# Where the loads of the third batch's keys and values stand in the queue of SP

## The chip, the core and the metric

The kernel runs on one core of a Trainium2 chip. The core has a TensorE for matmuls (PE in the profile, PEld for its weight loads), a VectorE (DVE), a ScalarE (ACT), a GpSimd (POOL), and SyncE (SP), which here does nothing but issue DMAs. Each engine runs its own list of instructions in order and waits on semaphores for the others. The metric is the device time of one execution in microseconds (us), lower is better; the time of a kernel is the median over its runs.

## What is computed

Two blocks in a row. The first is an attention with polynomial features: for each of 4 batches and 4 heads, 1088 tokens of 32 numbers; the second is a mixture of 4 experts, each of two weight matrices with a relu between, over the 4352 tokens that the first one leaves.

```python
def phi(x):                                   # 32 numbers -> 64 features
    a = np.einsum('rd,bhsd->bhsr', S1, x)     # S1, S2: 8 x 32
    b = np.einsum('rd,bhsd->bhsr', S2, x)
    return np.einsum('bhsi,bhsj->bhsij', a, b).reshape(*x.shape[:-1], 64)

q_p, k_p = phi(q), phi(k)
kv = np.einsum('bhsf,bhsd->bhfd', k_p, v)     # over all tokens of a batch
z = np.sum(k_p, axis=2)
attn = np.einsum('bhsf,bhfd->bhsd', q_p, kv) / (np.einsum('bhsf,bhf->bhs', q_p, z)[..., None] + 1e-06)
x = attn.transpose(0, 2, 1, 3).reshape(4352, 128)

p = domain_probs / (domain_probs.sum(-1, keepdims=True) + 1e-09)
out = sum(p[:, e:e+1] * (np.maximum(x @ w1[e], 0) @ w2[e]) for e in range(4))
```

## The kernel before

**The main loop is the mixture.** The 4352 tokens are cut into chunks (128, 448, 512, then seven of 448, and 128 at the end). For each chunk the loop at the end of the kernel goes through 16 steps: 4 experts times 4 pairs of blocks of the inner dimension; step `i` is step `i % 16` of chunk `i // 16`. A step has two halves, and a half step of an ordinary chunk is three matmuls into one PSUM bank (L1135, L1136, and L1186, between which ScalarE rescales the bank, L1137), the relu on ScalarE (L1189 or L1194), and second matmuls that are due by then (L1235, L1254). In the last step of an expert the sum is taken out of PSUM by VectorE, multiplied by the gate on GpSimd (L1293, L1295), and the next gate row is loaded into one of two buffers (L369, mostly on SP's queue).

**The attention is spread into that loop.** The queries of a batch are cut into units (first batch: 128, 448 and 512 tokens; third: 448, 448, 192). `lay_plan` (L817) writes a list of pieces with estimated costs, which the loop works off as the steps leave room. For a unit the pieces are:

- a transpose of its queries (L580);
- its projection, `unit_project` (L756): a few matmuls, a copy on ScalarE (L771), a write of the result to DRAM (`qd`, two DMAs, L773), and loads that read it back with rows repeated, as factors `qp` (L780) and `qb`. In the first batch each `qb` is loaded by four DMAs of 32 partitions each (L785), in later ones by one DMA (L782);
- the products of the factors on VectorE (`unit_product`, L791; L794), two per unit;
- the visit (`unit_visit`, L796): first the projection of the next unit, and then this unit's matmuls of products and key sums on TensorE;
- inverse, scale and a transpose to `y` on VectorE, a store of it to DRAM (`xd`, four DMAs, L728) and a load from there into `ring` (L737), where the mixture's next chunk reads its tokens; ScalarE and VectorE split these into parts (L909, L912).

In this list the third unit of the first batch is the first one made this way. Its factors are loaded in the order qp, four qb, qp, four qb.

**The keys of a batch** are pieces too (`key_pieces`, L512): transposes of `kn` (L396, L401), projections, additions (`summed`, with a copy of the values `vn` by `value_copy`), and products. `kn` and `vn` have one buffer each. `load_batch` (L137) issues the loads of the next batch's rows into them on SP's queue: one DMA of 544 KB for k, and for v four of 128 KB and two of 16 KB. The first batch is loaded at the start; the second at step 5 of the loop; the third from the last `summed` of the second batch's keys, and the fourth from that of the third's. The second batch's keys are worked on while the first chunks of the mixture run, so the third batch's load stands in SP's queue directly behind the ten DMAs of the third unit's factors, and ahead of a gate load and of the next unit's write to `qd`.

All of these DMAs are issued by SP in the order in which the program is written out. A DMA takes the eight completion semaphores in turn, and before it is issued it waits until the DMA that had the same semaphore, eight places before, has landed.

Of the kernel before, what the change touches and what calls it, by code (L numbers as in the profile page):

```python
# [24 lines left out]
def kernel(  # L25
# [28 lines left out]
    B, H, S, D = q.shape  # L54
# [48 lines left out]
    def psum(pool, tag):  # L103
        return pool.tile([P, 512], F32, tag=tag, name=tag)


    def load_rows(src, b, name, part=slice(0, S)):

        d = kn if name == "kn" else qn
        if b not in d:  # L110
            d[b] = lpool.tile([P, S], F32, tag=name, name=name)
        c, n = part.start, part.stop - part.start
        base = src.offset + b * H * S * D
        if name == "qn" and b == B - 1:
            for c, n, t in ((0, (G - 4) * D, 0), ((G - 4) * D, 4 * D, S - P)):
                nc.sync.dma_start(d[b][:, c : c + n], bass.AP(src.tensor, base + t * D, [[S * D, H], [n, 32], [1, n]]))
        else:
            nc.sync.dma_start(d[b][:, part], bass.AP(src.tensor, base + c, [[G * D, P], [1, n]]))  # L118

    def load_v(b):  # L120
        t = lpool.tile([P, H * NT * D], F32, tag="vn", name="vn")
        base = v.offset + b * H * S * D
        for a in range(4):
            nc.sync.dma_start(
                _ap(t, 32 * a, 32, 0, [[8 * D, H], [1, 8 * D]]),
                bass.AP(v.tensor, base + 8 * a * D, [[G * D, 32], [S * D, H], [1, 8 * D]]),
            )
        for a in range(2):
            nc.sync.dma_start(
                _ap(t, 32 * a, 32, 1024, [[D, H], [1, D]]),  # L130
                bass.AP(v.tensor, base + (32 + a) * D, [[G * D, 32], [S * D, H], [1, D]]),
            )
        return t
# [3 lines left out]
    def load_batch(b):  # L137
        load_rows(k, b, "kn")
        vn[b] = load_v(b)
# [254 lines left out]
    def key_turn(b, r, t0=0, n=4):  # L394
        if r < 2:
            nc.vector.transpose(  # L396
                _ap(kT, 0, P, 512 * r + P * t0, [[P, n], [32, 4], [1, 32]]),
                _ap(kn[b], 0, P, P * r + 32 * t0, [[32, n], [8 * D, 4], [1, 32]]),
            )
        else:  # L400
            nc.vector.transpose(kT[:, 1024:S], kn[b][:, 1024:S])  # L401

    def value_copy(b):
        copy = nc.gpsimd.tensor_copy if b == 1 else nc.scalar.copy
        for r in range(2):
            copy(
                vx[:, 4 * r : 4 * r + 4, :, 0:D].rearrange("p t h d -> p h t d"),
                _ap(vn[b], 0, P, P * r, [[8 * D, H], [D, 4], [1, D]]),
            )
            yield  # L410
        copy(vx[0:64, 8, :, 0:D], _ap(vn[b], 0, 64, 1024, [[D, H], [1, D]]))
# [21 lines left out]
    def key_project_wide(b, gi, kf):  # L433

        t0, n = FG[gi]
        if gi == 0:
            fss[b] = apool.tile([P, 2, NT, 32], F32, tag="fs", name="fs")
            kps[b] = apool.tile([P, NT, 2, P], F32, tag="kp", name="kp")
        for t in range(n):
            nc.tensor.matmul(  # L440
                kf[:, P * t : P * t + P], kT[:, P * (t0 + t) : P * (t0 + t + 1)], sk[:, :], start=True, stop=True
            )
        nc.scalar.copy(
            _ap(fss[b], 0, P, 32 * t0, [[32 * NT, 2], [32, n], [1, 32]]), _ap(kf, 0, P, 0, [[32, 2], [P, n], [1, 32]])
        )

    def key_add(b, gi, kf):
        t0, n = FG[gi]
        fs = _ap(fss[b], 0, P, 32 * t0, [[32 * NT, 2], [32, n], [1, 32]])
        nc.vector.tensor_tensor(out=fs, in0=_ap(kf, 0, P, HP, [[32, 2], [P, n], [1, 32]]), in1=fs, op=ALU.add)  # L450

    def key_product(b, t0, n, p, x, eng, kf=None):

        if b:
            fs = lambda k, dims: _ap(fss[b], 0, P, 32 * (NT * p + t0) + R2 * x + k, [[32, n]] + dims)
            eng.tensor_tensor(
                out=_ap(kps[b], 0, P, 256 * t0 + P * p + R * x, [[256, n], [R2, R], [1, R]]),
                in0=fs(0, [[1, R], [0, R]]), in1=fs(R, [[0, R], [1, R]]), op=ALU.mult,
            )
            return  # L460
        src, off = (kf, P * p) if kf is not None else (fss[b], 32 * (NT * p + t0))
        eng.tensor_tensor(  # L462
            out=_ap(kps[b], 0, P, 256 * t0 + P * p + 64 * x, [[256, n], [32, 2], [R, 4], [1, R]]),
            in0=_ap(src, 0, P, off + 4 * x, [[32, n], [R2, 2], [1, 4], [0, R]]),
            in1=_ap(fss[b], 0, P, 32 * (NT * p + t0) + R, [[32, n], [R2, 2], [0, 4], [1, R]]),
            op=ALU.mult,
        )
# [37 lines left out]
    def held(x):  # L505
        holds[0] += 1
        return x

    def free(n=1):
        holds[0] = max(0, holds[0] - n)  # L510

    def key_pieces(b):  # L512

        for r in range(3):
            add(0.69 if r < 2 else 0.23, lambda r=r: key_turn(b, r), f"turn{r}")
        values, kf = value_copy(b), {}

        def project(gi):
            kf[gi] = held(psum(ps_h, "h"))
            key_project_wide(b, gi, kf[gi])  # L520

        def summed(gi):
            key_add(b, gi, kf[gi])
            free()
            next(values, None)
            if gi == 2 and b + 1 < B:
                load_batch(b + 1)

        for gi in range(3):
            add(0.1, lambda gi=gi: project(gi), f"project{gi}", (f"turn{gi}", 2))  # L530
            add(0.2 if gi == 2 else 0.42, lambda gi=gi: summed(gi), f"sum{gi}", (f"project{gi}", 1))
        for p in range(2):
            for x in range(2):
                add(0.76, lambda p=p, x=x: key_product(b, 0, NT, p, x, nc.vector), "products")
# [278 lines left out]
    def add(cost, run, name, after=None):  # L813

        plan.append((cost, run, name, after))
# [597 lines left out]
    for i in range(len(steps) + LA):  # L1413
        if i < len(steps):
            m, kq = steps[i]
            until_there(START[m] + CHUNKS[m])
            rate = max(
                [0]
                + [
                    (needed[c] - spent[0]) / max(sum(rooms[2 * i : 2 * NQ * c - (EARLY if c > 1 else 13)]), 0.3)  # L1420
                    for c in range(m + 1, NC)
                    if 2 * NQ * c - (EARLY if c > 1 else 13) > 2 * i
                ]
            )

            def work():

                now[0] += 1
                if not NQ <= i < NQ + 2:
                    credit[0] = min(credit[0] + rate * rooms[min(now[0], len(rooms) - 1)], 0.5)  # L1430
                if holds[0]:
                    credit[0] = max(credit[0], 0.01)
                while credit[0] > 0:
                    cost = piece()
                    credit[0] -= cost
                    if not cost:
                        break
                for part in at_half.get(now[0] - 1, ()):
                    part()

            first(i, work, lambda j: behind(2 * i + j))
            to_due(i)
            if kq == NQ - 4 and 0 < m < NC - 2:
                until_there(START[m + 1] + CHUNKS[m + 1])
            for part in to_part.get(i, ()):
                part()
            if i == 2:
                gate_quotients()
            elif i == 8:
                later_weights()  # L1450
            elif i == 5:
                load_batch(1)
            elif i == 12:
                gate_rows()
            elif i == 13:
                later_mask()
                store_gates(range(1))
            elif i in (18, 20):
                load_gates(1, [(i - 18) // 2], nc.gpsimd)
            elif 14 <= i < 14 + B - 1:  # L1460
                store_gates(range(i - 13, i - 12))
            if m == NC - 2 and kq == NQ // 2:
                until_there(B * S)
                load_last()
        if i == LA:

            made_hp[3] = psum(ps_h, "h")
            for c in (0, HP):
                half_columns(3, made_hp[3], c)
        if NQ * (NC - 1) <= i < NQ * (NC - 1) + 2:  # L1470
            continue
        if not behind(2 * i + 1):
            next(ending, None)
# [29 lines left out]
```

## Time and profile before

| | us |
|---|---|
| median of 3 runs | 450.82 |
| lowest and highest run | 450.54, 452.36 |
| the profiled execution | 452.65 |
| its span, from the first instruction to the last | 450.9 |
| idle time of TensorE in the span | 7.9 |

TensorE's granted clock was 1.000 over the whole span. A profile gives, for each engine, its busy time, and ahead of an instruction the idle time of its engine with the thing that ended it. A wait for several semaphores is put down to the one that came last by the profile's reckoning, which can be wrong between DMAs. The DMA rows show when SP issued a DMA, not when its data landed.

This is SP's queue from the projection of the third unit's factors to the ring load of the same unit; columns: start in us, us taken, engine, line, operation, tiles (to <- from), count.

```profile
34.76 1.16 SPq L773 DMA_DIRECT2D qd<-qs  x2
35.96 0.58 SPq L118 DMA_DIRECT2D qn<-in_q_dram  x1
37.53 0.58 SPq L780 DMA_DIRECT2D qp<-qd  x1
38.16 2.64 SPq L785 DMA_DIRECT2D qb<-qd  x4
40.85 0.57 SPq L780 DMA_DIRECT2D qp<-qd  x1
41.46 3.38 SPq L785 DMA_DIRECT2D qb<-qd  x4
...
53.76 1.46 SPq L773 DMA_DIRECT2D qd<-qs  x2
56.89 0.58 SPq L780 DMA_DIRECT2D qp<-qd  x1
57.52 0.64 SPq L782 DMA_DIRECT2D qb<-qd  x1
58.28 0.54 SPq L780 DMA_DIRECT2D qp<-qd  x1
58.86 0.59 SPq L782 DMA_DIRECT2D qb<-qd  x1
60.15 1.75 SPq L728 DMA_DIRECT2D xd<-y  x4
65.12 0.34 SPq L737 DMA_DIRECT2D ring<-xd  x1
```

Between the two groups stand k and v of the third batch and one gate load.

### The profile page before, as it was taken

How to read it: one execution, taken by the hardware profiler on the slowest of the kernel's cores; microseconds unless marked ns; L12 is line 12 of the kernel's file. 1: busy time of each engine (PE TensorE's matmuls, PEld its weight loads, DVE VectorE, ACT ScalarE, POOL GpSimd, SP SyncE). 2: the span in 40 equal slices, each digit the busy share in tenths (PEclk: the TensorE clock that was granted, in tenths of full speed). 3: DMA queues.
4: the chain of work that ended last, by engine and by line, in shares of the span. 5: the costliest groups of instructions: out<-in, count | busy, mean ns of one | idle time of the engine just before them, and what ended most of it. 6: DMA issues, size and time to landing. Idle time of an engine off the chain costs nothing.

```text
span 450.9 us, 8672 instructions
## 1 busy us (share of the span) xinstructions
PE 443.0 (98%) x3021; PEld 369.0 (82%) x3021; DVE 359.5 (80%) x608; ACT 332.2 (74%) x702; POOL 122.1 (27%) x211
## 2 busy tenths in 40 slices
PE   8999899999999999999999999999999999999996
PEld 5887678777778888888888888888888888888885
DVE  5998689887988896889889868787788787876742
ACT  4478678677877876788687777887788788888831
POOL 7356123211323141212312402134123212322320
PEclk9999999999999999999999999999999999999999
DMA  6956741014223403242241152410321021027301
GB/s 196 309 133 172 164 141 32 26 36 122 93 59 87 119 23 81 52 126 74 72 118 23 22 130 65 119 43 21 95 62 30 22 47 39 22 42 253 113 4 28
DMA packets 53620, 38.47 MB, mean 85 GB/s; under 512 B 26920, under 2 KB 49640, under 8 KB 53576
## 3 DMA queue, kind: packets, MB, share of 16 engines
q1 hardware_dynamic: 52776, 37.31, 31.2%
q0 software_dynamic: 576, 0.53, 0.6%
q8 instruction: 24, 0.39, 0.4%
q14 instruction: 20, 0.16, 0.1%
q10 hardware_dynamic: 224, 0.07, 0.1%
HBM read 32.68 MB, written 5.21 MB: 84 GB/s over the span
## 4 chain that ended last, share of the span: by engine, by line
PE 92%; DMA 4%; DVE 3%; SPq 0%; issue 0%; ACT 0%; DVEq 0%; ACTq 0%
PE o L1254 40%; PE h L1186 13%; PE h L1135 13%; PE h L1136 13%; PE h L245 7%; PE o L245 3%; DMA vn<-in_v_dram 2%; DMA qb<-qd 2%; PE o L1235 2%; PE h L440 1%; DVE qp L593 1%; DVE qa L884 0%; DVE rd L625 0%; DVE kp L462 0%; SPq L118 0%
## 5 line engine op out<-in xcount | busy, mean ns | idle before, releaser
L1137 ACT ACTIVATE h<-h 128x448 f32<-128x448 f32 (+1 forms) x288 | 155.4, 540 | 79.0 <-PE h L1136 74.3
L1163 DVE SCALAR_TENSOR_TENSOR hb<-h,ha 128x448 fp32r<-128x448 f32 (+1 forms) x204 | 125.8, 624 | 54.7 <-ACT ha L1189 53.6
L1135 PE MATMUL h<-xa,wa 128*128 128x448 f32 (+1 forms) x288 | 134.6, 467 | 0.0
L1166 DVE SCALAR_TENSOR_TENSOR hd<-ha,hb 128x896 fp32r<-128x896 f32 (+1 forms) x102 | 116.4, 1141 | 8.2
L1189 ACT ACTIVATE ha<-h 128x448 fp32r<-128x448 f32 (+1 forms) x204 | 111.6, 547 | 0.0
L1186 PE MATMUL h<-xd,wd 128*128 128x448 f32 (+1 forms) x288 | 107.1, 372 | 0.1
L1136 PE MATMUL h<-xb,wb 128*128 128x448 f32 (+1 forms) x288 | 106.0, 368 | 0.0
L1293 POOL TENSOR_TENSOR ev<-ev,gate 128x256 f32<-128x256 f32 (+1 forms) x54 | 41.4, 768 | 220.0 <-DVE ev L1286 201.3
L1254 PE MATMUL o<-ha,vab 128*128 128x448 f32 (+1 forms) x204 | 76.4, 374 | 0.0
L1135 PEld LDWEIGHTS h<-xa,wa 128*128 128x128 f32 x288 | 54.2, 188 | 19.8 <-issue 15.2
L1136 PEld LDWEIGHTS h<-xb,wb 128*128 128x128 f32 x288 | 54.2, 188 | 19.3 <-issue 15.4
L1254 PE MATMUL o<-hid,w_sb 128*128 128x448 f32 (+1 forms) x136 | 62.9, 544 | 0.0
L1186 PEld LDWEIGHTS h<-xd,wd 128*128 128x128 f32 x288 | 54.0, 187 | 9.4 <-ACT h L1137 2.1
L1254 PE MATMUL o<-hd,vd 128*128 128x448 f32 (+1 forms) x204 | 58.8, 369 | 0.0
L1254 PE MATMUL o<-hb,vb 128*128 128x448 f32 (+1 forms) x136 | 49.8, 368 | 0.0
L1194 ACT ACTIVATE hid<-h 128x448 f32<-128x448 f32 (+1 forms) x84 | 46.4, 553 | 0.9 <-PE h L1186 0.8
L1295 POOL TENSOR_TENSOR total<-total,ev 128x256 f32<-128x256 f32 (+1 forms) x54 | 45.0, 833 | 4.2
L1254 PEld LDWEIGHTS o<-ha,vab 128*128 128x128 f32 x204 | 38.3, 188 | 4.2 <-issue 0.2
L1254 PEld LDWEIGHTS o<-hd,vd 128*128 128x128 f32 x204 | 38.1, 188 | 3.5
L1293 POOL TENSOR_TENSOR total<-ev,gate 128x256 f32<-128x256 f32 (+1 forms) x18 | 12.2, 698 | 74.8 <-issue 57.2
L1254 PEld LDWEIGHTS o<-hid,w_sb 128*128 128x128 f32 x136 | 25.6, 188 | 2.3
L1254 PEld LDWEIGHTS o<-hb,vb 128*128 128x128 f32 x136 | 25.5, 188 | 2.0
(142 smaller groups left out, 438.1 us busy)
## 6 DMA issues: line engine op xcount, KB each, us to landing
gate<-gates SPq DMA_DIRECT2D x22, 224.0 KB
kn<-in_k_dram SPq DMA_DIRECT2D x4, 544.0 KB
vn<-in_v_dram SPq DMA_DIRECT2D x16, 128.0 KB
w_last<-in_moe_w_dram SPq DMA_DIRECT2D x4, 512.0 KB
w_sb<-in_moe_w_dram SPq DMA_DIRECT2D x3, 512.0 KB
w_sb<-in_moe_w_dram SPq DMA_DIRECT2D x6, 256.0 KB
qp<-qd SPq DMA_DIRECT2D x6, 224.0 KB
qb<-qd SPq DMA_DIRECT2D x6, 224.0 KB
```

The costliest lines, as they stand in the source:

```text
L245: nc.tensor.matmul(out(s), weights(s), moving(s), **flags)
L1135: nc.tensor.matmul(g, wa[:, e, w], xa, start=True, stop=False)
L1136: nc.tensor.matmul(g, wb[:, e, w], xb, start=False, stop=True)
L1137: nc.scalar.activation(g, g, ACTF.Copy, scale=1.0 + R12)
L1163: nc.vector.scalar_tensor_tensor(out=hb, in0=g, scalar=0.0, in1=high, op0=ALU.max, op1=ALU.subtract)
L1166: nc.vector.scalar_tensor_tensor(out=d2, in0=a2.bitcast(F32), scalar=R12, in1=b2.bitcast(F32), op0=ALU.mult, op1=ALU.subtract)
L1186: nc.tensor.matmul(g, w, x, start=False, stop=True, skip_group_check=True)
L1189: nc.scalar.activation(ha, g, ACTF.Relu, scale=NEAR)
L1194: nc.scalar.activation(hid[i][j], g, ACTF.Relu)
L1254: nc.tensor.matmul(acc[m, e][o][:, 0:n], w, h, start=first_one, stop=last)
L1293: nc.gpsimd.tensor_tensor(out=to[:, x], in0=ev[:, x], in1=g[:, x], op=ALU.mult)
L1295: nc.gpsimd.tensor_tensor(out=total[m][:, x], in0=total[m][:, x], in1=ev[:, x], op=ALU.add)
```

## The change

The load of the third batch's rows is taken out of the keys' pieces and issued from the loop, at step 24. The fourth batch's load stays where it was, in the third batch's keys.

```diff
@@ -523,7 +523,7 @@
             key_add(b, gi, kf[gi])
             free()
             next(values, None)
-            if gi == 2 and b + 1 < B:
+            if gi == 2 and 1 < b < B - 1:
                 load_batch(b + 1)
 
         for gi in range(3):
@@ -1450,6 +1450,8 @@
                 later_weights()
             elif i == 5:
                 load_batch(1)
+            elif i == 24:
+                load_batch(2)
             elif i == 12:
                 gate_rows()
             elif i == 13:
```

Written out, SP's queue changes in one place: the seven DMAs of the third batch's k and v come twelve places later, behind one gate load, the two writes and four loads of the next unit's factors, the four stores of `y` and the ring load, and ahead of the three gate loads that follow. The instructions of the other engines stay in the same order with the same shapes; they wait for other counts of the DMA semaphores.

## The prediction

> **What bounds the kernel now.** First the busy times (part 1 of the page), then the waits between engines, then the chain that ended last and the queue of SP around the one wait that the chain shows, and last the stretches of one us there.
>
> ```profile
> PE 443.0 (98%) x3021; PEld 369.0 (82%) x3021; DVE 359.5 (80%) x608; ACT 332.2 (74%) x702; POOL 122.1 (27%) x211
> ...
> PE h L245 <- POOL sr L298: 1.3, 1, 1.3
> ...
> PE h L245 <- DVE qp L794: 1.1, 1, 1.1
> ```
>
> TensorE is busy for 98% of the span of 450.9 us, so only what fills one of its gaps, or opens a new one, moves the end. The list of waits has four columns of meaning: who waited, for whom, us in total, times, longest. Two waits of TensorE are over 1 us: 1.3 us at the start, which this change doesn't reach, and 1.1 us before matmuls of L245 for a product on VectorE (L794). Behind 54 us no wait of TensorE itself of over 0.1 us is listed. The 1.1 us is thus about all that work in the queues can win.
>
> Where that product's own time goes stands in the chain of waits:
>
> ```profile
> 42.11 8.26 DMA qb<-qd
> ...
> 50.38 2.08 DMA vn<-in_v_dram
> 52.47 0.70 DVE qp L794
> ...
> 53.21 0.69 PE h L245 x16
> ```
>
> The chain names a v load as the last releaser. The product reads qp and qb only, and the orders of SP's queue say what truly came last. SP uses eight DMA semaphores in turn, so each DMA is issued once the one eight places before it has landed. The unit's factors are qp, qb 1 to 4, a second qp and qb 5 to 8 (64 KB each qb), then comes k. So k here stands eight places behind qb 2, and each v one further:
>
> ```profile
> 45.12 0.35 SPq L118 DMA_DIRECT2D kn<-in_k_dram  x1
> ...
> 45.77 0.37 SPq L124 DMA_DIRECT2D vn<-in_v_dram  x1
> ...
> 47.82 0.31 SPq L124 DMA_DIRECT2D vn<-in_v_dram  x1
> ...
> 52.43 0.35 SPq L369 DMA_DIRECT2D gate<-gates  x1
> ```
>
> Read as landings of the DMA eight places before, with the issues between them that the same timeline has (46.97, 48.89, 50.38, 51.65): qb 2, 3 and 4 by 45.12, 45.77 and 46.97; the second qp at 47.82; qb 5 to 8 at 48.89, 50.38, 51.65 and 52.43. The product begins at 52.46, when qb 8 is there. So the last 64 KB of factors are late, not v. The steps between landings tell more: 0.65 us from qb 2 to qb 3, before any row of k moves, and (52.43 - 47.82) / 4 = 1.15 us for each of the last four, while k and v move.
>
> ```profile
> 45.00:46.00 1.00, 1.00 (x5) 1.00 0.27 102
> 46.00:47.00 1.00, 1.00 (x7) 1.00 0.95 177
> ...
> 49.00:50.00 1.00, 1.00 (x5) 1.00 1.14 165
> 50.00:51.00 1.00, 1.00 (x8) 1.00 1.09 191
> ```
>
> The last two columns are the DMA engines' mean busy share and GB/s. From 45 to 46, with qb alone, 0.27 of 16 engines (4.3 of them) move 102 GB/s. From 46 on the share is about 1 or over, yet at 49 to 51 only 165 to 191 GB/s flow: every packet takes longer.
>
> **The change part by part.** SP's program keeps its 179 rows; seven of its DMAs move: k (544 KB), four of v (128 KB) and two of v (16 KB), 1.09 MB in all, from behind qb 8 to behind the store and the ring load of the same unit. Orders and shapes of the instructions of the other four engines stay. No DMA or wait is added.
>
> (a) *The place that they leave.* The last factors must now travel without 1.09 MB beside them. At the 102 GB/s of the row for 45 to 46, one qb (65,536 B) takes 0.64 us, which is the 0.65 us seen there between landings. Slow bound: the second qp lands at 47.82 as before, and four qb follow at 0.65 us: 47.82 + 2.6 = 50.42. Fast bound: from 45.77 on there remain qb 4, the quarter of the second qp (256 KB) that lies on the same four engines if it is spread evenly (64 KB), and qb 5 to 8, six times 64 KB or 393 KB, which at 102 GB/s take 3.86 us: 49.63. If k and v cost the factors nothing, 52.43 stays; that is the bound on the other side. I take 50.4, the slower of the two without k and v: part of what held the loads up to 47.82 may have been the second qp and not k.
>
> What has to be met: TensorE ends its first half of the visit's matmuls at 52.11 (1.10 us before 53.21), and the product needs 0.75 us from its start (52.46) to TensorE's (53.21). So the product must begin by 51.36. At 50.4 it is there 0.9 us early, and TensorE's wait of 1.10 us is gone whole: **-1.10 us**. Each us by which qb 8 comes later than 51.36 gives one back.
>
> VectorE's 3.5 us of idle time before the product shrinks to some 1.5 us, and its next items (weight splits, L912) start up to 2 us earlier; TensorE doesn't wait for them (the wait list has none), so this is worth nothing.
>
> (b) *The DMAs that move up.* The gate load of L369, which SP issued at 52.43, now waits for POOL to free its tile: POOL's product with the older gate runs from 49.02 to 50.30, so it is issued near 50.35. The query write of the next unit (L773) waits for ScalarE's copy, which ends at 52.04; it was issued at 53.76 and 54.73, and now goes at about 52.1 and 52.7. Its factors (L780, L782) follow about 2 us earlier than 56.89. Their product comes at 96.49, so none of this is on the path: 0.
>
> (c) *The place where they go.* Without the 1.10 us the store of y (60.15) comes at 59.05, and the ring load (65.12) at 64.0 at the latest. Then k and v: seven issues of 0.31 to 0.37 us, 2.3 us, with waits for DMAs that have long landed; SP is free again at about 67. Behind them stand three gate loads. The first went at 65.57 and goes at 67 to 68; it lies behind 1.09 MB, which took 46 to 52 us before, 6 us, so it lands by about 74. POOL reads that gate at 84.07: 10 us of cover. The first transpose of this k (L396) starts at 111.24, some 39 us after the rows land near 72. Cost: 0. Without that cover VectorE, and then TensorE, would wait out the difference.
>
> What remains close is the ring load itself, now just ahead of k. ScalarE splits it at 68.82 (L909), and the wait list has 0.3 us for it. With everything 1.1 us earlier it is wanted at 67.7. The ring load is over about 68.0 (the DMA share falls from 0.78 at 67 to 68 to 0.08 at 68 to 69), 2.9 us after its issue at 65.12; issued at 64.0 it is there at 66.9, 0.8 us early. Cost 0, since TensorE didn't wait for the 0.3 us before; the other bound is the last rival below.
>
> (d) *After the visit* TensorE's chain has two third-part matmuls (L1186) of 0.47 and 0.46 us, at 55.92 and 57.55, against 0.20 elsewhere; both wait for ScalarE's L1137. ScalarE's own wait (3.3 us) ends with TensorE's L1136 at 55.26, which comes behind the visit with or without the stall. So I keep them: 0, at best -0.53 us.
>
> The sum: -1.10 + 0 + 0 + 0 = -1.1 us on the profiled span of 450.9 us: 449.8. The profiled execution as a whole was 452.65, 1.75 us around its span, and stays so; the timed median (450.82) is close to the span by chance, 1.83 below that execution. The change of 1.1 us is taken off the median: **449.7 us**.
>
> A rule speaks against (a): the Trainium skill, "DMA: Bandwidth & Descriptors", section "Queues, rings and completion order", has each DMA engine consume a queue's descriptors in ring order. By it k and v, issued later on the same queue, can't go ahead of qb, qb 8 would land at 52.43 again, and the time would stay at 450.8. The trace bears that order out only in part: k is indeed issued behind every qb, yet the steps between landings grew from 0.65 to 1.15 us once it moved. That case is the first rival.
>
> **The rivals.**
>
> *The factors were late anyway.* The eight qb of 64 KB share few engines (4.3 busy at 45 to 46), and the queue in front of them is the same. If their landings spread out for their own sake, qb 8 lands at 52.43 again and the wait moves nowhere: 450.8. For it: k and v are issued behind qb on one queue, and qb 3 to qb 4 took 1.20 us with k hardly begun. Against it: 0.65 us before, up to 1.49 us with v, and a share over 1 for 165 GB/s.
>
> *More than the wait comes back.* The two late matmuls in (d) recover too: 1.10 + 0.53 = 1.63 us, 449.2. For it: they stand directly behind the stall. Against it: ScalarE there waits for TensorE, not for the product.
>
> *Slower: the ring load shares its time with k and v.* The place is ScalarE's split at 67.7, which is in order before copies that TensorE needs. If k and v slow the ring as they slowed qb (1.15 / 0.65, 1.8 times), 2.9 us become 5.1: 69.1, 1.4 us late, of which ScalarE's idle time per half-step (0.4 to 0.5 us by its timeline) hides 0.45: some 1.0 us lost, and the gain is all but gone (450.7). A ring that lands behind 67.7 + 0.45 + 1.1 = 69.25 makes the kernel slower than before. At the worst it ends with the 6 us of k and v, at 66.9 + 6 = 72.9: the split is 5.2 us late, TensorE loses 4.75, and the time is 450.8 - 1.1 + 4.75 = 454.5, which I give this case. Against it: the ring is issued first, and the 900 KB of the next unit's factors, beside which its four stores (xd) landed in 3 us, now go earlier than the stores.
>
> **How the numbers follow.** Forecast 0.70; late anyway 0.15; more than the wait 0.08; slower 0.07. About 0.5% (2.25 us, so 448.6 and 453.1) is what a measurement of this kernel can tell from no change, the three runs of before lying 0.4% apart. The forecast and the first two rivals (449.2 to 450.8) all lie within it; the last is at or over its edge. With measuring on both sides that makes same 0.87, faster 0.05, slower 0.08. The range runs from 448.7 (the larger gain and 0.5 us of spread) to 451.4 (no gain and 0.6 us of spread).
>
> **What would show it.** Right: no wait of L245 for L794 in the list; SP's gate load near 50.4; L794's second product at 49.7 to 51.3 in the window; TensorE's L1235 behind the visit 1.1 us earlier (52.7 for 53.82); the ring load issued by 64.0 and landed before ScalarE's split. Wrong: L794 still at 52.4; a wait of ScalarE at L909 of over 0.5 us near 67.7, and TensorE waiting at L1186 behind it; a new wait of POOL for the gate at 83, or of VectorE at L396 near 110.

## The result, and the profile after

| | before | after |
|---|---|---|
| median of 22 runs each | 451.12 us | 450.12 us |
| lowest to highest | 449.69 to 452.69 | 449.62 to 451.43 |
| median span | 449.1 (29 runs beside the first four experiments) | 448.2 (the 22 runs) |
| profiled execution, its span | 452.65, 450.9 | 450.1, 448.1 |

The ratio of the changed kernel to the one before is 0.9981, with a 95% interval of 0.9972 to 0.999. That is 0.86 us of 451.12, with an interval of 0.45 to 1.26; the medians themselves lie 1.00 us apart. So the gain is clear of zero, but less than the 0.5% that the prediction took for what can be told from no change. The 1.10 us of the prediction lie in the interval. One execution of the changed kernel, beside a later experiment, took 552.51 us at a granted clock of 0.754, and the ratios leave it out.

The two profiles are 2.8 us apart, three times as much. They are followed here from the visit on. First the waits of the changed kernel from 45 to 60 us (engine and line, what it waited for, us in total, times, longest):

```profile
DVE vd L912 <- ACT vab L909: 1.8, 1, 1.8
...
DVE qp L794 <- DMA qb<-qd: 1.3, 1, 1.3
```

TensorE's matmuls (PE) are not in it: the wait of L245 for L794 is gone. VectorE (DVE) still waits for the factors, but 1.3 us where it was 3.5, and with time to spare. The weight splits of L912 (`vd`), which now start earlier, wait longer for ScalarE, 1.8 us where it was 0.8. VectorE's own timeline says when the second product begins (start, us, then in brackets the idle time before it and what ended it):

```profile
50.34 0.69 DVE L794 TENSOR_TENSOR qp<-qp,qb 128x512 f32<-128x512 f32 x1 [1.26 <-DMA qb<-qd]
```

50.34, where before had 52.46. In the table of stretches (TensorE's busy share, granted clock; the last two columns are the DMA engines' mean share and GB/s) the factors now travel alone:

```profile
46.00:47.00 1.00, 1.00 (x5) 1.00 0.26 98
...
48.00:49.00 1.00, 1.00 (x5) 1.00 0.24 90
49.00:50.00 1.00, 1.00 (x6) 1.00 0.08 29
```

About four of 16 engines are busy (0.26 x 16 = 4.2) at some 98 GB/s, and the load is over in the stretch that begins at 49. Before, the share was 1.05 to 1.14 from 47 to 51. SP's queue shows what moved and what came up behind it:

```profile
50.48 0.35 SPq L369 DMA_DIRECT2D gate<-gates  x1
52.21 1.14 SPq L773 DMA_DIRECT2D qd<-qs  x2
54.86 0.58 SPq L780 DMA_DIRECT2D qp<-qd  x1
...
63.31 0.34 SPq L737 DMA_DIRECT2D ring<-xd  x1
63.69 0.43 SPq L118 DMA_DIRECT2D kn<-in_k_dram  x1
64.17 1.85 SPq L124 DMA_DIRECT2D vn<-in_v_dram  x4
66.06 0.91 SPq L129 DMA_DIRECT2D vn<-in_v_dram  x2
67.09 0.35 SPq L369 DMA_DIRECT2D gate<-gates  x1
```

The ring load goes 1.8 us earlier than before (65.12), and k and v go behind it. ScalarE splits the ring at 67.65 without a wait. On the chain of waits (start, us, what) the matmuls that stood behind the stall run straight on:

```profile
50.88 1.84 PE h L245 x40
52.72 0.95 PE o L1235 x2
...
54.75 0.47 PE h L1186
```

L1235 begins at 52.72, where before had 53.89. TensorE's stream ran 0.15 us later in this execution ahead of the visit, and here it is 1.17 us ahead, so up to here it gained 1.3 us: the wait of 1.10 and some small drift. At its last matmuls it is 1.47 us ahead (L245's group at 444.72 for 446.19). The other 1.3 us of the 2.8 lies behind all computation. The last transfers of the kernel before, by stretches (VectorE's share, then the same columns):

```profile
447.00:448.00 1.00, 0.00 (x0) 1.00 0.17 46
448.00:449.00 1.00, 0.00 (x0) 1.00 0.13 34
449.00:450.00 1.00, 0.00 (x0) 1.00 0.02 2
```

and of the changed one:

```profile
446.00:447.00 1.00, 0.00 (x0) 1.00 0.22 66
447.00:448.00 1.00, 0.00 (x0) 1.00 0.00 0
```

In the first the last store (L1227, issued at 447.01) still moves data at 449.0, 2 us later; in the second (issued at 445.53) it is over within about 1.5 us. That is one late store in one execution and not the change: two more profiles of the unchanged kernel, below, end like the changed one and have a span of 449.3. So the profile that the sum was made on was a long execution, and the change is worth what the medians say.

### The profile page after: what moved, and what is told of

It reads as the page before. It is cut to its first block, busy times and chain, and to the rows that moved or that the text cites. A ratio compares the mean times of both kernels' runs of the same rounds, so it can differ in the third digit from the quotient of the medians.

```text
span 448.1 us, 8673 instructions
## 1 busy us (share of the span) xinstructions
PE 442.8 (99%) x3021; PEld 369.2 (82%) x3021; DVE 359.8 (80%) x608; ACT 332.1 (74%) x702; POOL 122.2 (27%) x211
## 4 chain that ended last, share of the span: by engine, by line
PE 95%; DVE 2%; DMA 1%; issue 0%; SPq 0%; ACT 0%; DVEq 0%; ACTq 0%
PE o L1254 40%; PE h L1186 14%; PE h L1135 13%; PE h L1136 13%; PE h L245 7%; PE o L1235 3%; PE o L245 3%; DMA vn<-in_v_dram 1%; PE h L440 1%; DVE qp L593 1%; DVE qa L884 0%; DVE rd L625 0%; DVE kp L462 0%; SPq L118 0%; DVE qf L873 0%
## 5 line engine op out<-in xcount | busy, mean ns | idle before, releaser
L1186 PE MATMUL h<-xd,wd 128*128 128x448 f32 (+1 forms) x288 | 107.1, 372 | 0.1
L1186 PEld LDWEIGHTS h<-xd,wd 128*128 128x128 f32 x288 | 54.0, 188 | 9.3 <-ACT h L1137 2.1
L1194 ACT ACTIVATE hid<-h 128x448 f32<-128x448 f32 (+1 forms) x84 | 46.4, 553 | 0.9 <-PE h L1186 0.8
```

Of the source, the lines that this page charges most:

```text
L1186: nc.tensor.matmul(g, w, x, start=False, stop=True, skip_group_check=True)
L1194: nc.scalar.activation(hid[i][j], g, ACTF.Relu)
```

## The experiments

One measure goes through them: the time from the issue of the unit's first qp (37.53 in before, 37.68 in after) to the start of L794's second product. It is 14.93 us before and 12.66 after. By the trace of before, TensorE waits once it is over 52.11 - 0.75 - 37.53 = 13.83 us. SP doesn't always take the same time to issue the factors, so a second measure counts from the issue of the last four qb (41.46 in before, 41.61 in after). The edits are shown against the changed kernel; added lines shift its line numbers by 2 to 11, so L794 appears as L796 to L805.

That the product waits for the last qb, and not for the v load that the profile names, has support in five profiles: the gate load, which stands eight places behind qb 8, is issued 0.03 us ahead of the product in all three of before (52.43 for 52.46, 52.18 for 52.21, 52.38 for 52.41) and in the last two kernels of the table (53.04 for 53.07, 51.71 for 51.74).

| kernel | qp to product, us | last qb to product, us | wait of L245, us | median, us | ratio to before (95%) |
|---|---|---|---|---|---|
| before, three profiles | 14.93, 14.91, 14.81 | 11.00, 11.00, 10.77 | 1.10, 1.10, 0.99 | 451.1 | 1 |
| changed | 12.66 | 8.73 | 0 | 450.12 | 0.9981 (0.9972 to 0.999) |
| two loads over 16 engines | 13.71 | 9.78 | 0 | 451.04 | 1.000 (0.999 to 1.0009) |
| the same on 4 engines | 12.64 | 8.73 | 0 | 459.56 | 1.019 (1.0168 to 1.0213) |
| k stays, v moves | 13.08 | 9.14 | 0 | 450.00 | 0.9986 (0.9975 to 0.9996) |
| v stays, k moves | 12.98 | 9.07 | 0 | 450.24 | 0.9985 (0.9974 to 0.9996) |
| both stay, on GpSimd's queue | 17.86 | 13.94 | 4.04 | 456.19 | 1.0116 (1.0092 to 1.014) |
| step 23, ahead of the ring | 13.16 | 8.62 | 0 (6.12 at L1186) | 456.22 | 1.0106 (1.0083 to 1.0129) |
| step 36 | 12.72 | 8.79 | 0 | 450.27 | 0.998 (0.9968 to 0.9992) |
| long rows in pieces | 15.54 | 11.29 | 1.72 | 453.08, one run | |
| v ahead of k | 14.08 | 10.14 | 0.27 | 450.53, one run | |

In four of these kernels no other load runs on the other engines beside the last factors (changed, the loads on 4 engines, step 23, step 36). Their first measure spreads over 12.64 to 13.16 us, because at step 23 SP took 1.20 us to issue the second qp, where the other three took 0.57 to 0.59. Their second measure spreads over 8.62 to 8.79 only, and that of the unchanged kernel over 10.77 to 11.00. Each of the other rows is a single profile, so differences of less than 0.3 us between rows mean nothing.

**Do other bytes delay the factors, and from which engines?** Both kernels load k and v at step 24 as the changed one does. At the old place they issue two more loads of 544 KB, of k's memory, into the same tiles; step 24 overwrites them. They differ in how these loads are spread.

```
+    def two_loads(b):
+        base = k.offset + b * H * S * D
+        for tag, width in (("kn", S), ("vn", H * NT * D)):
+            t = lpool.tile([P, width], F32, tag=tag, name=tag)
+            nc.sync.dma_start(t[:, 0:S], bass.AP(k.tensor, base, [[G * D, P], [1, S]]))
...
+            if gi == 2 and b == 1:
+                two_loads(2)
```

> The real loads of the third batch stay at step 24. At their old place stand two loads of 544 KB instead, spread over all 16 DMA engines, into the same tiles, whose contents are overwritten at step 24 (so the bytes are loaded twice). Theory (bytes of k and v beside the factors slow them): the second product of L794 starts at 51.6 to 53 and TensorE waits 0.4 to 1.7 us for it. Rival (the number of DMAs or what v does alone was the cause): it starts near 50.4 as in the changed kernel and TensorE doesn't wait.

In the second kernel the source is `[[0, 4], [G * D, 32], [1, S]]`: 32 rows read four times, with an outer dimension of 4, as the qb loads have one.

> The same two loads of 544 KB at the old place, but with a source that repeats 32 rows four times as qb's does, so that they should go to the same few DMA engines as qb, behind it. If the engines work in the order of the queue and it was the traffic of the other engines that slowed the factors: the second product starts at 50.2 to 50.7, no wait of TensorE. If later loads take time from earlier ones on the same engine: it starts at 52 or later, a wait of 0.8 us or more. The next unit's factors then queue behind 1.09 MB on few engines, so the ring load may come late and cost some us of its own near 68.

The stretches and the product of the first, over 16 engines:

```profile
46.00:47.00 1.00, 1.00 (x5) 1.00 0.96 329
47.00:48.00 1.00, 1.00 (x6) 1.00 1.03 283
48.00:49.00 1.00, 1.00 (x6) 1.00 1.05 288
```

```profile
51.00 0.69 DVE L802 TENSOR_TENSOR qp<-qp,qb 128x512 f32<-128x512 f32 x1 [2.32 <-DMA qb<-qd]
```

And of the second, on 4:

```profile
47.00:48.00 1.00, 1.00 (x5) 1.00 0.27 100
48.00:49.00 1.00, 1.00 (x5) 1.00 0.26 96
```

```profile
50.42 0.69 DVE L802 TENSOR_TENSOR qp<-qp,qb 128x512 f32<-128x512 f32 x1 [1.32 <-DMA qb<-qd]
```

Behind the factors on the same engines, the 1.09 MB cost them nothing (12.64 for 12.66). Spread over all 16, the same bytes cost 1.05 us. So the delay comes with the traffic on the other engines. What the transfers share on their way isn't shown. The delay was less than the 2.25 us that k and v themselves cost, though, and the product is ahead of the 13.83 at which TensorE waits: it was expected at 51.6 to 53 and came at 51.00. The first kernel's median time was that of before nevertheless, although TensorE has no wait at the product. Its profiled execution has a span of 448.3 us, about the changed kernel's 448.1, but took 451.23, so that 2.9 us lie around its span, where the runs of the changed kernel have 1.7 to 2.6. Its median span (448.65) is 0.45 us below before's and 0.45 above the changed kernel's; that rest wasn't traced to a place.

The second kernel lost its time elsewhere:

```profile
ACT xa L917 <- DMA ring<-xd: 7.3, 1, 7.3
...
PE h L1194 <- ACT h L1145: 7.3, 1, 7.3
```

At some 98 GB/s on four engines the two loads take about 11 us and hold up everything behind them on SP's queue:

```profile
52.24 1.16 SPq L781 DMA_DIRECT2D qd<-qs  x2
62.92 0.56 SPq L788 DMA_DIRECT2D qp<-qd  x1
...
72.50 0.34 SPq L745 DMA_DIRECT2D ring<-xd  x1
```

The next factors go 8 us later than in the changed kernel, the ring 9.2 us, and ScalarE's split of the ring (L917) waits 7.34 us, TensorE's L1194 behind it 7.25 us. So a late ring does stop TensorE in the way that the third rival says; what makes it late here is the traffic ahead of it in the queue. Of the 8.6 us that its median lies above before, that wait less the 1.10 us won gives 6.15. Some 1.6 of the other 2.4 us are TensorE's clock: the trace has it at 0.50 from 73 to 79, so that the work from 76.24, when TensorE goes on, to about 79.4 takes twice its time. The rest wasn't placed.

**Which of the two loads is it?** One stays at the old place, the other moves to step 24.

```
+            if gi == 2 and b == 1:
+                load_rows(k, 2, "kn")
...
-                load_batch(2)
+                vn[2] = load_v(2)
```

> Only v moves to step 24, k (544 KB, one DMA) stays at its old place. Theory: half the bytes, of which most move before 49, so the second product starts at 50.7 to 51.6 and TensorE waits 0 to 0.3 us; time within 0.1% of the changed kernel. Rival (k alone is the cause): 52.0 to 52.5, wait 0.7 to 1.1 us.

The mirror image keeps `vn[2] = load_v(2)` at the old place and has `load_rows(k, 2, "kn")` at step 24.

> Only k moves to step 24, v (six DMAs, 544 KB) stays at its old place. Before the change the steps between landings were longest (1.49 and 1.27 us) while v moved. Theory: the second product starts at 51.2 to 52.2 and TensorE waits 0 to 0.8 us. Rival (k alone is the cause): 50.4, no wait.

k alone costs the factors 0.42 us, v alone 0.32 (0.41 and 0.34 by the second measure), both together 2.25: the costs don't add up. Both products came earlier than expected, at 50.42 for 50.7 to 51.6 and at 50.60 for 51.2 to 52.2, so the theory that priced them by their bytes had them too high. Either alone leaves the product 0.75 us or more within its limit, and both kernels have the changed one's time.

**How much do executions of the unchanged kernel differ?** Two more profiles of it, with no edit.

> The kernel before, unchanged, for a second profile. If the landing of the factors differs from execution to execution, TensorE's wait for L794's second product differs from 1.10 us: I expect 0.5 to 1.3 us, and the last store at the end without the 1.3 us that one part of it came late in the first profile, so a span of 449 to 449.6.

> The kernel before once more: as the run ahead of it, wait 0.5 to 1.3 us, span 448.8 to 449.8. With the first profile these give the spread of the wait that the change removes.

Spans 449.3 and 449.3; products at 52.21 and 52.41; waits 1.10 and 0.99. The wait is in all three profiles, and within 0.12 us of the same size. The last matmuls began 1.2 us later than in the changed kernel (445.92 and 445.96 for 444.72), which is the whole difference of the spans, 449.3 - 448.1 = 1.2.

**Does another queue keep k and v out of the factors' way?** Both at the old place, issued by GpSimd.

```
+            if gi == 2 and b == 1:
+                load_rows(k, 2, "kn", queue=nc.gpsimd)
+                vn[2] = load_v(2, queue=nc.gpsimd)
...
-            elif i == 24:
-                load_batch(2)
```

> The third batch's k and v stay at the old place in the program but are issued by GpSimd's queue, from about 41 us on, so that they run beside the factors on the same engines and not behind them on SP's queue. If a DMA engine takes turns between queues, the four busy engines must carry some 68 KB each of k and v before qb 8 is done, 2.6 us at their rate: the second product at 52.5 to 53.5, TensorE waits 1.1 to 2.1 us, time 0.1 to 0.3% above the changed kernel's 450.1. Rival (what matters is only that they are over early): 50.3 to 51.3, no wait.

```profile
DVE qp L797 <- DMA qb<-qd: 6.4, 2, 4.6
...
PE h L245 <- DVE qp L797: 4.0, 1, 4.0
```

Worse than before, and by more than expected (a wait of 1.1 to 2.1 us): 17.86 us to the second product, which comes at 55.39, and TensorE waits 4.04 us. On SP's queue k and v stood behind the factors on the four engines that both use, and there they cost nothing in the kernel with the loads on 4 engines. Here GpSimd issued them from 40.44 on, among the factors and 4.7 us earlier than SP did before. The run doesn't tell apart what the other queue and what the earlier issue did. The Trainium skill, "DMA: Bandwidth & Descriptors", section "Queues, rings and completion order", says that a DMA engine goes round between the queues that it has work for, packet by packet; these 17.86 us agree with it in direction. The 2.6 us that the expectation reckoned from such turns don't reach the 5.2 us that the factors lost. The wait is 2.9 us longer than before's, and the median is 5.1 us higher. Some 1.7 of the other 2.2 us are again TensorE's clock, at 0.50 from about 56.6 to 60.0.

**Is the place behind the ring what matters, and how much would it cost ahead of it?** The load goes one step earlier, behind the next unit's factors.

```
-            elif i == 24:
-                load_batch(2)
...
+            if i == 23:
+                load_batch(2)
```

> k and v of the third batch one step earlier than in the changed kernel (step 23), which puts them behind the next unit's factors and ahead of the four stores of y and the ring load. Queue order: the stores land behind 1.09 MB, the ring load is issued near 67 and lands near 69.7, ScalarE's split waits 1.5 to 3 us and TensorE loses 1 to 3 us near 69: 451.2 to 453.2. Rival (k and v are spread thin enough): ring load at 64 to 65, no wait of ScalarE over 0.5 us, time as the changed kernel's.

```profile
58.02 0.33 SPq L118 DMA_DIRECT2D kn<-in_k_dram  x1
...
64.94 3.53 SPq L728 DMA_DIRECT2D xd<-y  x4
71.35 0.34 SPq L737 DMA_DIRECT2D ring<-xd  x1
```

```profile
ACT xa L909 <- DMA ring<-xd: 6.2, 1, 6.2
PE h L1186 <- ACT h L1137: 6.1, 1, 6.1
```

The store of y is issued 6 us later than in the changed kernel and the ring 8 us, more than the expectation had (a ring load near 67, a loss of 1 to 3 us for TensorE); ScalarE waits 6.23 us, TensorE 6.12. Behind that wait TensorE's clock is down (TensorE's busy share, granted clock, then the DMA engines' share and GB/s):

```profile
75.00:76.00 1.00, 0.83 (x2) 0.50 0.00 0
...
80.00:81.00 1.00, 1.00 (x6) 0.88 0.00 0
81.00:82.00 1.00, 1.00 (x5) 1.00 0.00 0
```

TensorE goes on at 75.17 and has half its clock in every stretch until about 80.2, which costs it 2.5 us more. The wait less the 1.10 us won, and this, make 7.5 us, and the span of this execution (456.9) is 7.6 us above that of the unchanged kernel (449.3). It was the longest of the five, 459.87 us; the medians differ by 5.1 us, so the others lost less. One step in the program turns the gain of 0.2% into a loss of 1.1%.

In these traces every long wait of TensorE behind 45 us has such a stretch: 7.25, 6.12, 4.04 and, with long rows below, 1.72 us of waiting were each followed by 3 to 5 us of work at 0.50. Behind the 1.10 us of before the clock stays at 1.00. Where between 1.10 and 1.72 us this begins, and whether it always does, no run shows. So TensorE pays twice for a transfer that is very late.

**Is it the new place, or that the old one is left?** The load goes to step 36.

```
-            elif i == 24:
+            elif i == 36:
```

> The load of k and v at step 36 instead of 24, behind three more gate loads and four output stores, some 15 us later. If the gain comes from the place that they leave and the new place is free: second product of L794 at 50.0 to 50.7, no wait of TensorE, time within 0.1% of the changed kernel (449.9 to 450.4), no wait of VectorE at L396 near 110. Rival (the new place matters): a time over 450.6 or a new wait of TensorE.

k is issued at 94.47 instead of 63.69, the product is as early (12.72), and the ratio is the same. The gain lies in leaving the old place. Beside it the changed kernel ran once more:

> The changed kernel, unchanged, beside the run above on one chip: 449.9 to 450.4, ratio to the kernel before 0.997 to 0.999, product at 50.0 to 50.7 and no wait of TensorE for it.

Ratio 0.9967 (0.9954 to 0.9981) in these rounds, just under the expected 0.997, median 450.09; the two intervals overlap. The start of its product isn't known.

**Why do k and v cost more than two whole loads of the same bytes?** First, rows: seven loads at the old place with the sizes and partitions of k and v, but the 128 KB pieces with rows of 4 KB of k's memory in place of v's short ones; overwritten at step 24.

```
+        load_rows(k, b, "kn")
+        t = lpool.tile([P, H * NT * D], F32, tag="vn", name="vn")
+        for a in range(4):
+            nc.sync.dma_start(t[32 * a : 32 * a + 32, 0:1024], bass.AP(k.tensor, base + 32 * a * G * D, [[G * D, 32], [1, 1024]]))
...
```

> At the old place stand seven loads of the same sizes and into the same partitions as k and v (544 KB, four of 128 KB into 32 partitions each, two of 16 KB), but every row of the 128 KB pieces is one run of 4 KB in DRAM and not four of 1 KB; the real loads follow at step 24. The product's start counted from the issue of the first qp was 14.9 us with k and v, 13.7 with two loads of 544 KB, 12.7 with none. If v's short runs of 1 KB make up the difference: 13.5 to 14.0, TensorE waits 0 to 0.2 us. If it is that the pieces stand one after the other in the queue: 14.6 to 15.1, wait 0.8 to 1.2 us.

```profile
DVE qp L805 <- DMA qb<-qd: 4.1, 1, 4.1
...
PE h L254 <- DVE qp L805: 1.7, 1, 1.7
```

15.54 us: not better than before (14.8 to 14.9) but 0.6 us worse, and a wait of 1.72 us. About half of the 0.6 is that SP issued the second qp in 0.92 us where it mostly takes 0.57; by the second measure it is 11.29 for 10.77 to 11.00, about the same. Short rows are not the cause. Then, the order: real loads at the old place, v's six ahead of k, and none at step 24.

```
+                vn[2] = load_v(2)
+                load_rows(k, 2, "kn")
```

> Old place, old loads, but v's six DMAs ahead of k. If what runs beside the last factors sets the loss, k's long rows now do: 13.3 to 14.0 us from the first qp's issue, TensorE waits 0 to 0.2 us. If only the sum of bytes counts: 14.6 to 15.1, wait 0.8 to 1.2 us.

14.08 us and a wait of 0.27, just over the 13.3 to 14.0 expected: the order of the same seven loads is worth 0.7 to 0.9 us. So at one place, with about the same bytes over 16 engines and by the second measure, two whole loads cost 1.05 us, pieces ahead of k 1.4, k ahead of pieces 2.0 to 2.3 and k ahead of pieces with long rows 2.6. All but the third of these four are single profiles. That pieces behind k cost most is shown; why they do is not.

None of these kernels beat the changed one. In it, TensorE idles for some 0.6 us in all behind the first 8 us, so this direction holds nothing more.

## Why the prediction was right, by its steps

- *(a) The place that is left.* The product was forecast at 50.4 and begins at 50.34. The wait is gone whole, and TensorE gained its 1.10 us. The fast bound (49.63) wasn't reached. The four engines and their rate (0.26, 98 GB/s) carried the sum. The reason for taking the slow bound, a second qp that lands at 47.82 even without k and v, can't be read from this profile, where no issue of SP waits for that landing; so how close the 50.4 came is in part luck.
- *(b) The DMAs that move up.* Gate at 50.48 (50.35 forecast), query write at 52.21 (52.1), factors at 54.86, 2 us earlier. No wait came of them.
- *(c) The place where they go.* Ring issued at 63.31 (64.0 at the latest), gate at 67.09 (67 to 68), split at 67.65 with no wait. POOL's product with the gate at 82.9 and the transpose of k (L396) near 110 have no wait for a DMA. One reading was wrong without harm: the 0.3 us in the wait list for L909 belong to an earlier split, between 20 and 40 us, and end with a write of `ring` by VectorE (L722). The split at 68.82 had no wait.
- *(d) The late matmuls.* 0.47 and 0.46 us at 54.75 and 56.39, as before. The second rival, that they recover too, falls.
- *The sum.* 1.10 us forecast; the ratio gives 0.86, with an interval that holds 1.10. The 449.7 us forecast for the median became 450.12, since with 22 runs before's own median is 451.12 and not 450.82. What was off was what the sum was taken from: the profiled execution of before was 1.8 us longer than the median of later spans, 1.3 us of it that one late store. The text called the nearness of its span to the timed median chance, and it was: time and span of one run of the changed kernel differ by 1.7 to 2.6 us, and before's median span is 449.1. Taking the change off the median, not off the profile, kept that out of the number.
- *"The factors were late anyway"* falls: with k and v elsewhere they land 2 us earlier, wherever these go (8.73 at step 24, 8.62 at step 23, 8.79 at step 36, from the last four qb). The rule behind it, ring order on one queue, isn't wrong. It holds on an engine, as the two loads on four engines show (12.64). What it doesn't cover is that the loads also run on twelve engines that the factors don't use, and slow them from there.
- *"The ring load shares its time with k and v"* didn't come: with k issued 0.4 us behind the ring load, the split has no wait. What the step earlier shows is a neighbour of it: with k and v ahead of the stores and the ring in the queue, the ring is 8 us late. From there on the chain is the rival's, a late split and then TensorE, but it costs more than the 4.75 us given: 6.1 us of wait and 2.5 us at half the clock in that execution. The working had no term for the clock, and one wrong size: ScalarE was to hide 0.45 us of a late split, and it hid 0.1 (7.34 to 7.25, 6.23 to 6.12).

## What to carry to other kernels

A background load isn't harmless because it is issued behind the transfer that matters: look at the steps between landings before and after it starts, and at how few engines the urgent transfer has. Before moving it, list what the queue holds at each possible place and when each of these is wanted; one step earlier cost five times what the move wins. Where the wait at a worse place is long, look at the granted clock behind it too. A gain the size of the run-to-run spread should be taken off the median, and from a wait that several profiles of the old kernel show.

## What the runs showed of the hardware

- A transfer on about four of the 16 DMA engines was slowed by transfers on the others: 1.05 us for 1.09 MB over 16 engines, nothing for the same amount queued behind it on its own four.
- The delays don't add up: 0.42 us for k, 0.32 for v, 2.25 for both, and 1.4 when v goes first.
- After waits of TensorE of 1.72 to 7.25 us its granted clock was 0.50 for the next 3 to 5 us of work; after the wait of 1.10 us it stayed at 1.00.
- The Trainium skill, "DMA: Bandwidth & Descriptors", section "Why a DMA increments its semaphore by 16 and not by 1", has a transfer split over the largest number up to 16 that divides the outer dimensions of both sides. With an outer dimension of 4, the share of 0.26 of 16 agrees (4.2 engines), and its price is 98 GB/s where the load over 16 had 283 to 329 in all.
- Issuing the same background loads from GpSimd's queue cost the urgent transfer 5.2 us more than having them at a later place on SP's (17.86 for 12.66); they were also issued 4.7 us earlier than before.
